# Spectral buffers lent to the end stage and to the second chunk pair, constant loads on SyncE's queue, and six free banks before a visit

## The chip, the cores and the metric

The kernel runs on one core of one Trainium2 chip. The time is device microseconds of one execution of the program, as the median over several runs. TensorE is called PE here, VectorE DVE, ScalarE ACT, GpSimd POOL and SyncE SP.

## What is computed

```python
g = sigmoid((q * gate_w).sum(-1, keepdims=True))
k_shift = causal convolution of k with 4 taps per channel
y = irfft(rfft(k_shift * v, 2S) * rfft(ssm_k, 2S))[:S] + k_shift * v * ssm_D
a = q * y
b = relu(q @ w1) @ w2
out = g * a + (1 - g) * b        # S = 2048, D = 512, DFF = 1792, float32
```

## The kernel before

Every float32 factor of the MLP is split into a high and a low part in the reduced format fp32r, and every product takes three matmuls (high by high, low by high, high by low). These are the dense matmuls: 128 x 128 weights against 512 columns. The 14 blocks of 128 hidden units are worked off in three eras (0 to 4, 5 to 9, 10 to 13), and in each era the 2048 rows go through in four chunks of 512. In the last era the chunks are taken in pairs (`combine(p, c, d, ...)`, chunks 0 and 1 for p = 0, chunks 2 and 3 for p = 1) and the first product of the MLP is done by a scheme with seven block products in place of eight; it needs sums and differences of the raw x of both chunks (`t1` to `t4`, on DVE), for which four pieces `b11`, `b12`, `b21`, `b22` of raw x are loaded, and `b22` a second time (`again`).

The long convolution is a two-stage Fourier transform. Its first stage (`stage1`, small-tile matmuls `s1h` and `s1x`) stores to the DRAM buffer `sa`. The middle (`conv_mid`) handles eight groups g: it loads `r_h` and `r_x` from `sa`, transforms both (`f_h`, `f_x`, 32 small-tile matmuls each in two halves of two PSUM banks), multiplies them on DVE into the spectral buffers `p`, `ha`, `qa`, `qb`, and adds the parts on POOL (`sums`, tile `p`; for g = 7 and part of g = 6 on DVE). The inverse `iv` of a group stands at the head of the visit two groups later and fills four banks; ACT copies these to `bv`, and SP stores them to the DRAM buffer `sb`. ACT also copies two of the four banks of `f_h` into `ha`. A visit is one such uninterrupted run of small-tile matmuls on PE between dense ones. The end (`conv_end`) is four more visits of 32 matmuls, `cy`, each in two halves; a half reads one pair of row blocks, loaded from `sb` into two `br` tiles of 512 KB each. DVE then forms g times q times `cy` (`after`) and adds the MLP's part (`finish`), and SP stores `out`.

The order of the instructions on each engine, and of the DMA issues on SP, is fixed when the program is built, by a list scheduler (`Plan`) with cost numbers of its own. Two of its rules matter here. A tile is given out from a counted set per tag (`room`), so that a load into a tag waits for whoever gave the buffer back. PSUM has eight banks, tag `cv`; the first link of a visit is taken only when `need` banks are free (`NEEDM`, five for every group g), or after it has waited `PATIENT` = 20 of the planner's microseconds. On the chip none of this is looked at again: an instruction waits only on the semaphores of the instructions whose data or buffers it uses.

SBUF is shared out by phases. Pool `cp1` serves stage one, `phase(2)` opens a pool with the spectral buffers (`p`, `ha`, `qa`, `qb`, `cf`, `cc`, `bv`), and `phase(3)`, which comes when all stores to `sb` and all gates are done, closes it and opens the pool with the `br` and `xs` tiles. `xs` holds the raw x of the second chunk pair.

The gates are computed by `gates`: a load of q, `tensor_tensor_reduce` with the gate weights `gwt` (in a `qb` buffer) and a scratch output `j` (in a `qa` buffer), and a sigmoid for eight row blocks at a time. Two constants, `s1t` (for stage one) and `ibt` (for `cy`), are loaded by DMAs that POOL issues at the start.

Of the kernel before, what the change touches and what calls it, by code (L numbers as in the profile page):

```python
# [11 lines left out]
OP = mybir.AluOpType  # L12

S, D, DFF = 2048, 512, 1792
P = 128
# [242 lines left out]
def dve_time(n):  # L258
    return n * 0.001042 + 0.12
# [3 lines left out]
TILES = 0.865  # L263
SWITCH = 0.19
ROW = P * D * 4


def build(tc, wf, xp, qn, kn, vn, hn, dn, sh, gw, w1, w2, cs1, ccf, cci, cib, out):
    nc = tc.nc
# [15 lines left out]
    room = {"raw": RAW, "x": 4, "cv": 8, "hh": HB, "cc": BEHIND + 1, "cf": 2, "qa": 1, "qb": 1, "acc": ACC, "tmp": TMP, "ev": EV, "r": RB,  # L285
            "ha": HAB, "p": PB, "bv": BVB, "j": 1, "w1": WA, "w2": WB, "br": BR, "xs": 4}
    plan = Plan(room)
# [135 lines left out]
    def combine(p, c, d, cgate):  # L423
        pairs = [tuple(ERAS[2][2 * u:2 * u + 2]) for u in range(2)]
        rank = (1, XR[p])
        tag = "xs" if p else "r"
        pool_of = lambda: cpool[0] if p else mp
        raws, made = {}, {}
        for nm, src, k0 in (("b22", d, 2), ("b12", d, 0), ("b11", c, 0), ("b21", c, 2)):
            go = lambda nm=nm, src=src, k0=k0: nc.sync.dma_start(rows(tile_of(("xc", p, nm), tag, 2 * D, p=pool_of())), xp[src, k0:k0 + 2].rearrange("k p d -> p k d"))  # L430
            raws[nm] = add("SP", ISSUE, -47, go, [cgate if p else xgate[0]], [tag], dma=2 * ROW, fifo=[tag])

# [26 lines left out]
        def again():  # L459
            nc.sync.dma_start(rows(tile_of(("xc", p, "b22"), tag, 2 * D, p=pool_of())), xp[d, 2:4].rearrange("k p d -> p k d"))  # L460

        for nm, ld in (("t2", "t4"), ("t3", "t2"), ("t4", "t4"), ("t1", "t2"), ("b22", None)):
            if not ld:
                made[ld] = add("SP", ISSUE, -47, again, [made["t2"]], [tag], dma=2 * ROW, fifo=[tag])
            for i in range(2):
                cut(nm, i, made[ld], [tag] if i else [])

# [77 lines left out]
        for u in us:  # L545
            relu(d, pairs[u][0], n("Y", u), c12[u], ["cv"])
        begun[0] = (p5 if LATE[p] else y)[1]
        for s in range(4):
            mlp2(2, d, s, [pairs[u][e] for e in (1, 0) for u in us])

# [197 lines left out]
    sbstores = []  # L748
    ys, rtags = {}, {}

# [18 lines left out]
    def conv_mid(g, gate):  # L769
# [37 lines left out]
        for o in range(2):  # L807
            f = link(TILES, lambda o=o: rounds("h", o), deps, ["cv"] * 2 + ([] if o else ["ha"]), rtags[g, "h"] if o else ())
            fh.append(f)
        if not IV_FIRST:  # L810
            turned()
# [85 lines left out]
    def gates(gate):  # L897
        rank = (1, GATE)

        def weights():  # L900
            nc.sync.dma_start(tile_of(("gwt",), "qb", 2 * D)[:, :D], gw.partition_broadcast(P))

        def junk():
            tile_of(("j",), "qa", 2 * D)
            tile_of(("gs",), "gs", 48, p=mp)

        gwl = add("SP", ISSUE, GATE - 1, weights, ys[7], ["qb"], dma=ROW)
        j = add("SP", 0.0, GATE - 1, junk, ys[7], ["qa"])
        done = []
        for m in range(0, 16, GN):  # L910
            prev = [None]
            for n in order_n[m:m + GN]:
                if n % 2 == 0:
                    def load(n=n):
                        two = tile_of(("gq", n), "r", 2 * D, p=mp)
                        nc.sync.dma_start(rows(two), qn[:, n:n + 2])
                        T["q", n], T["q", n + 1] = two[:, :D], two[:, D:]

                    ld = add("SP", ISSUE, GATE, load, [gate], ["r"], dma=2 * ROW, fifo=["r"])

                def go(n=n):
                    nc.vector.tensor_tensor_reduce(T["j",][:, :D], T["q", n], T["gwt",][:, :D], op0=OP.mult, op1=OP.add, scale=1.0, scalar=0.0, accum_out=gs(0, n))

                prev.append(add("DVE", dve_time(D) + 0.08, rank, go, [ld, gwl, j, *prev[-1:]], port=True))
            a = add("ACT", 0.2, rank, lambda m=m: nc.scalar.activation(gs(1, order_n[m], GN), gs(0, order_n[m], GN), AF.Sigmoid), prev[-1:])
            a = add("DVE", 0.07, rank, lambda m=m: nc.vector.tensor_scalar(gs(2, order_n[m], GN), gs(1, order_n[m], GN), -1.0, 1.0, op0=OP.mult, op1=OP.add), [a])
            for n in order_n[m:m + GN]:
                gdone[n] = a
# [4 lines left out]
    def conv_end(ns, gate):  # L933
        ready = {}
        for n in ns:
            rank = (1, 700.0 + order_n.index(n))
            k = lambda nm, n=n: (nm, n)

            if n % 2 == 0:
                def ld(n=n):  # L940
                    for b in range(2):
                        src = sb[64 * b:64 * b + 64].rearrange("(i n c) k d -> n (c k) i d", i=2, c=2)
                        nc.sync.dma_start(rows(tile_of(("br", b, n), "br", 2 * D)), src[n:n + 2].rearrange("n q i d -> (n q) i d"))

                e = add("SP", 2 * ISSUE, rank[1], ld, [gate], ["br", "br"], dma=4 * ROW, fifo=["br"])
            ready[n] = [e, gdone[n]]
        chain = []
        deps = [ibload] + [r[0] for r in ready.values()]
        for m in range(len(ns) // 2):
            def go(two=ns[2 * m:2 * m + 2]):  # L950
                for n in two:
                    bank(("cy", n))

                for to in range(4):
                    for n in two:
                        at = slice(64 * (n % 2), 64 * (n % 2) + 64)
                        mm(T["cy", n][32 * to:32 * to + 32, :], T["ibt",][at, :], T["br", to % 2, two[0]][at, to // 2 * D:(to // 2 + 1) * D], start=True, stop=True)  # L957

            chain.append(add("PE", TILES, (0, 700.0 + ns[0]), go, deps if not chain else chain[-1:], ["cv"] * 2, ["br", "br"], tiles=True, need=0 if chain else NEED))
            for n in ns[2 * m:2 * m + 2]:  # L960
                after(n, chain[-1], ready[n][1])
        plan.chain(chain)
# [21 lines left out]
    for k in range(4):  # L984
        load_x(0, 0, k, -1000 + k)
        load_first(k, -1002.5 + k)
    s1ld = add("POOL", 1.04, 0, lambda: nc.gpsimd.dma_start(tile_of(("s1t",), "s1c", 64), cs1), [w, p1], dma=ROW // 4)
    ibload = add("POOL", 1.04, 5, lambda: nc.gpsimd.dma_start(tile_of(("ibt",), "ibt", 32, p=mp), cib), [s1ld], dma=ROW // 8)
    for f in ERAS[0][G:]:
# [42 lines left out]
    gates(m2[1, CHUNKS[1][-1], 1])  # L1032
    p3 = add("SP", 0.0, -1e3, lambda: phase(3), sbstores + [gdone[n] for n in order_n])
    combine(1, *CHUNKS[2][2:], p3)
    for m in range(0, 16, NE):
# [14 lines left out]
NEED, PATIENT = 4, 20.0  # L1050
NEEDM = {g: 5 for g in range(8)}
NE = 4
# [5 lines left out]
GATE = 690.0  # L1058
BR = 8
LATE = True, False  # L1060
GN = 8
BACK = 1.5
CUT = (0, -899), (0, -899)
XR = 525.0, 704.5
WA = 7
# [73 lines left out]
```

## Time and profile before

| what | value |
|---|---|
| time, median of 3 runs | 383.59 us (383.54 to 383.60) |
| the profiled execution | 383.29 us, its span 381.5 us |
| PE busy | 376.6 us, 99% of the span |
| DVE busy | 299.2 us, 78% |
| ACT busy | 169.9 us, 45% |
| POOL busy | 82.4 us, 22% |
| granted clock | 1.000 of full speed |
| moved by DMA | 98.53 MB, mean 258 GB/s |

The profile is of one execution, whose time includes 1.79 us outside the span that the trace covers. PE, DVE, ACT and POOL count as busy while they execute; issuing a DMA does not count. An engine below 99% need not be free when it is wanted, and an idle one costs nothing unless PE waits for it.

### The profile page before, as it was taken

What the parts mean: (1) busy time and instruction counts of PE and PEld (TensorE: products, weight loads), DVE (VectorE), ACT (ScalarE), POOL (GpSimd) and SP (SyncE); (2) the same over time, 40 slices, a digit from 0 to 9 for tenths busy, and PEclk for the clock granted to TensorE, in tenths of its full rate; (3) what the DMA queues carried; (4) which work ended last, traced back from release to release, by engine and by line L of the source; (5) the groups of instructions that cost most, each with busy time, mean ns of one, the idle gap of its engine ahead of it and who ended that gap; (6) DMA issues with size and microseconds to landing.
All of it is one profiled execution on the core that took longest, in us unless ns stands there. A gap on an engine that the chain in (4) does not pass through costs nothing.

```text
span 381.5 us, 6622 instructions
## 1 busy us (share of the span) xinstructions
PE 376.6 (99%) x2481; PEld 265.3 (70%) x2481; DVE 299.2 (78%) x387; ACT 169.9 (45%) x311; POOL 82.4 (22%) x67
## 2 busy tenths in 40 slices
PE   9999999999999999999999999999999999999995
PEld 5888866866866886786646644657468688858664
DVE  5698999699599963127879898879899895699762
ACT  5542365275346644514132453053347864655230
POOL 1000000000000000000898899978400000000000
PEclk9999999999999999999999999999999999999999
DMA  8987178958958959789688979985753789159812
GB/s 276 381 314 246 55 284 317 338 201 317 365 195 305 338 213 346 257 278 327 236 298 285 304 221 368 326 281 174 262 207 113 246 298 380 38 187 320 293 58 82
DMA packets 45298, 98.53 MB, mean 258 GB/s; under 512 B 4657, under 2 KB 7489, under 8 KB 45266
## 3 DMA queue, kind: packets, MB, share of 16 engines
q1 hardware_dynamic: 44914, 97.80, 72.9%
q8 instruction: 19, 0.31, 0.3%
q10 hardware_dynamic: 288, 0.26, 0.2%
q14 instruction: 13, 0.11, 0.1%
q0 software_dynamic: 64, 0.05, 0.1%
HBM read 67.68 MB, written 30.41 MB: 257 GB/s over the span
## 4 chain that ended last, share of the span: by engine, by line
PE 98%; DMA 1%; DVE 0%; ACT 0%; DVEq 0%; issue 0%
PE m L628 14%; PE m L629 13%; PE m L630 13%; PE m L412 9%; PE m L413 9%; PE m L414 9%; PE iv L865 4%; PE f_x L786 4%; PE f_h L786 4%; PE m L398 3%; PE s1x L673 2%; PE X L486 2%; PE cy L957 2%; PE X L487 2%; PE X L488 2%; PE s1h L673 2%
## 5 line engine op out<-in xcount | busy, mean ns | idle before, releaser
L628 PE MATMUL m<-w1h_h,hh 128*128 128x512 f32 x224 | 89.1, 398 | 0.0
L629 PE MATMUL m<-w1l_l,hh 128*128 128x512 f32 x224 | 87.3, 390 | 0.0
L630 PE MATMUL m<-w1h_h,hl 128*128 128x512 f32 x224 | 87.2, 389 | 0.0
L837 POOL TENSOR_TENSOR p<-p,ha 128x512 f32<-128x512 f32 x26 | 33.1, 1297 | 184.4 <-DVE ha L831 183.9
L628 PEld LDWEIGHTS m<-w1h_h,hh 128*128 128x128 f32 x224 | 42.0, 188 | 21.5 <-ACT ev L678 6.5
L602 ACT ACTIVATE hh<-m 128x512 fp32r<-128x512 f32 x40 | 23.6, 599 | 65.8 <-PE m L414 65.8
L630 PEld LDWEIGHTS m<-w1h_h,hl 128*128 128x128 f32 x224 | 42.0, 188 | 9.0
L629 PEld LDWEIGHTS m<-w1l_l,hh 128*128 128x128 f32 x224 | 42.1, 188 | 8.2
L605 DVE SCALAR_TENSOR_TENSOR hl<-m,hh 128x512 fp32r<-128x512 f32 x40 | 27.2, 686 | 24.5 <-ACT hh L602 24.5
L412 PE MATMUL m<-xh_h,w0h_h 128*128 128x512 f32 x96 | 37.7, 393 | 0.0
L413 PE MATMUL m<-xl_l,w0h_h 128*128 128x512 f32 x96 | 37.4, 389 | 0.0
L414 PE MATMUL m<-xh_h,w0l_l 128*128 128x512 f32 x96 | 37.4, 389 | 0.0
L875 ACT COPY bv<-iv 128x512 f32<-128x512 f32 x32 | 18.1, 598 | 40.3 <-PE iv L865 39.7
L643 ACT COPY y<-m 128x512 f32<-128x512 f32 x28 | 16.5, 590 | 38.5 <-PE m L630 38.2
L732 DVE TENSOR_TENSOR acc<-acc,tmp 128x1024 f32<-128x1024 f32 x24 | 29.4, 1224 | 0.8
L412 PEld LDWEIGHTS m<-xh_h,w0h_h 128*128 128x128 f32 x96 | 18.0, 188 | 6.2 <-issue 1.7
L729 DVE TENSOR_TENSOR tmp<-r,sht_sht 128x512 f32<-128x512 f32 x32 | 20.8, 684 | 0.2
L678 ACT COPY ev<-s1x 128x512 f32<-128x512 f32 x32 | 16.4, 600 | 9.4 <-PE s1x L673 9.4
L414 PEld LDWEIGHTS m<-xh_h,w0l_l 128*128 128x128 f32 x96 | 18.0, 188 | 3.8
L413 PEld LDWEIGHTS m<-xl_l,w0h_h 128*128 128x128 f32 x96 | 18.0, 188 | 3.6
L823 DVE TENSOR_TENSOR ha<-f_h,ha 128x512 f32<-128x512 f32 x16 | 10.6, 688 | 12.6 <-PE f_h L786 11.6
L837 POOL TENSOR_TENSOR p<-p,qa 128x512 f32<-128x512 f32 x14 | 20.3, 1466 | 0.0
(147 smaller groups left out, 659.9 us busy)
## 6 DMA issues: line engine op xcount, KB each, us to landing
sa<-ev SPq DMA_DIRECT2D x64, 256.0 KB, 3.0
r_h<-sa SPq DMA_DIRECT2D x16, 512.0 KB, 5.5
r_x<-sa SPq DMA_DIRECT2D x16, 512.0 KB, 6.8
sb<-bv SPq DMA_DIRECT2D x32, 256.0 KB, 2.6
br<-sb SPq DMA_DIRECT2D x16, 512.0 KB, 7.3
raw<-xp SPq DMA_DIRECT2D x28, 256.0 KB, 4.0
raw<-w SPq DMA_DIRECT2D x22, 256.0 KB, 3.9
r<-kn SPq DMA_DIRECT2D x10, 512.0 KB, 5.0
```

The source lines that it names most:

```text
L412: mm(ps, part("h", f, k), T["x", "h", xe, c, k], start=k == 0, stop=False)
L413: mm(ps, part("h", f, k), T["x", "l", xe, c, k], start=False, stop=False)
L414: mm(ps, part("l", f, k), T["x", "h", xe, c, k], start=False, stop=k == 3)
L602: nc.scalar.activation(tile_of(("hh", era, c, f), "hh", dt=F32R, p=mp, bufs=HB), T["m1", era, c, f], AF.Relu)
L605: nc.vector.scalar_tensor_tensor(tile_of(("hl", era, c, f), "hl", dt=F32R, p=mp, bufs=HB), T["m1", era, c, f], 0.0, T["hh", era, c, f].bit ...
L628: mm(ps, T["hh", era, c, f][:, z], T["w", "h", 1, f], start=f == fs[0] and not seeding, stop=False, skip_group_check=True)
L629: mm(ps, T["hh", era, c, f][:, z], T["w", "l", 1, f], start=False, stop=False, skip_group_check=True)
L630: mm(ps, T["hl", era, c, f][:, z], T["w", "h", 1, f], start=False, stop=f == fs[-1], skip_group_check=True)
L729: nc.vector.tensor_tensor(o[:, z], T["k", c + (j == 0) + part][:, u], T["sht",][:, j * D:(j + 1) * D], op=OP.mult)
L732: nc.vector.tensor_tensor(T["acc", c], T["acc", c], T[dst], op=OP.add)
L786: mm(ps[b][32 * j:32 * j + 32, :], T[k("cf")][at, 64 * j + 32 * o:64 * j + 32 * o + 32], T[k("r", t, j // 2)][at, (j % 2) * D:(j % 2 + 1) ...
L837: (nc.gpsimd if eng == "POOL" else nc.vector).tensor_tensor(planes("p", dst, n), planes("p", dst, n), planes(src, u, n), op=OP.add if sign ...
```

## The change

The pool of the spectral buffers is no longer closed before the end stage. The pairs of row blocks that `conv_end` loads go, in turn, into `p`, `p`, a buffer `bx` of its own, `p`, `p`, `bx`, `ha`, `ha`, and the raw x of the second chunk pair into the two `ha` tiles (two pieces each) and the second `b22` into `qa`; these loads are gated by group 7's `f_h` and not by `phase(3)`. The gate weights and the scratch output have tiles of their own. The two constant loads are issued by SP, and the scratch memory for DMAs that GpSimd describes is set to 2048. `NEEDM` is six. `EARLY` = 2, 2 takes the place of `LATE`: for both pairs, the first two of the four accumulators of the second chunk may be seeded from the earlier of two points.

```diff
@@ -283,7 +283,7 @@
 
 
     room = {"raw": RAW, "x": 4, "cv": 8, "hh": HB, "cc": BEHIND + 1, "cf": 2, "qa": 1, "qb": 1, "acc": ACC, "tmp": TMP, "ev": EV, "r": RB,
-            "ha": HAB, "p": PB, "bv": BVB, "j": 1, "w1": WA, "w2": WB, "br": BR, "xs": 4}
+            "ha": HAB, "p": PB, "bv": BVB, "j": 1, "w1": WA, "w2": WB, "bx": 1}
     plan = Plan(room)
     add = plan.add
     T = Tiles()
@@ -423,12 +423,22 @@
     def combine(p, c, d, cgate):
         pairs = [tuple(ERAS[2][2 * u:2 * u + 2]) for u in range(2)]
         rank = (1, XR[p])
-        tag = "xs" if p else "r"
-        pool_of = lambda: cpool[0] if p else mp
         raws, made = {}, {}
+        home = dict(b22=0, b12=0, b11=1, b21=1)
         for nm, src, k0 in (("b22", d, 2), ("b12", d, 0), ("b11", c, 0), ("b21", c, 2)):
-            go = lambda nm=nm, src=src, k0=k0: nc.sync.dma_start(rows(tile_of(("xc", p, nm), tag, 2 * D, p=pool_of())), xp[src, k0:k0 + 2].rearrange("k p d -> p k d"))
-            raws[nm] = add("SP", ISSUE, -47, go, [cgate if p else xgate[0]], [tag], dma=2 * ROW, fifo=[tag])
+            def go(nm=nm, src=src, k0=k0):
+                if not p:
+                    tile_of(("xc", p, nm), "r", 2 * D, p=mp)
+                else:
+                    if nm in ("b22", "b11"):
+                        tile_of(("xt", home[nm]), "ha", 4 * D)
+                    T["xc", p, nm] = T["xt", home[nm]][:, 2 * D * (nm in ("b12", "b21")):][:, :2 * D]
+                nc.sync.dma_start(rows(T["xc", p, nm]), xp[src, k0:k0 + 2].rearrange("k p d -> p k d"))
+
+            if p:
+                raws[nm] = add("SP", ISSUE, -47, go, [cgate, *raws.values()], ["ha"] if nm in ("b22", "b11") else (), dma=2 * ROW)
+            else:
+                raws[nm] = add("SP", ISSUE, -47, go, [xgate[0]], ["r"], dma=2 * ROW, fifo=["r"])
 
         def minus(dst, a, b, deps, into, sign=-1):
             def go(eng="DVE"):
@@ -457,13 +467,13 @@
         minus("t4", "b21", "t2", [made["t2"], raws["b21"], *own("b21")], "b21")
 
         def again():
-            nc.sync.dma_start(rows(tile_of(("xc", p, "b22"), tag, 2 * D, p=pool_of())), xp[d, 2:4].rearrange("k p d -> p k d"))
+            nc.sync.dma_start(rows(tile_of(("xc", p, "b22"), "qa" if p else "r", 2 * D, p=None if p else mp)), xp[d, 2:4].rearrange("k p d -> p k d"))
 
         for nm, ld in (("t2", "t4"), ("t3", "t2"), ("t4", "t4"), ("t1", "t2"), ("b22", None)):
             if not ld:
-                made[ld] = add("SP", ISSUE, -47, again, [made["t2"]], [tag], dma=2 * ROW, fifo=[tag])
+                made[ld] = add("SP", ISSUE, -47, again, [made["t2"], *(ys[7] if p else ())], ["qa" if p else "r"], dma=2 * ROW, fifo=() if p else ["r"])
             for i in range(2):
-                cut(nm, i, made[ld], [tag] if i else [])
+                cut(nm, i, made[ld], ["r"] if not p and i else {"t4": ["ha"], "t1": ["ha"], "b22": ["qa"]}.get(nm, []) if i else [])
 
         def x_at(b, nm, i):
             if not p and nm in ("b21", "b11"):
@@ -544,8 +554,8 @@
         c12 = [summed(n("Y", u), n("Y", u), n("u2", u), [y[u]], ["raw"]) for u in us]
         for u in us:
             relu(d, pairs[u][0], n("Y", u), c12[u], ["cv"])
-        begun[0] = (p5 if LATE[p] else y)[1]
         for s in range(4):
+            begun[0] = (p5 if s < EARLY[p] else y)[1]
             mlp2(2, d, s, [pairs[u][e] for e in (1, 0) for u in us])
 
     wpart = {}
@@ -746,7 +756,7 @@
 
 
     sbstores = []
-    ys, rtags = {}, {}
+    ys, rtags, fh7 = {}, {}, [None]
 
     def conv_load(g, gate):
         rank = 500.0 + 4 * g
@@ -807,6 +817,7 @@
         for o in range(2):
             f = link(TILES, lambda o=o: rounds("h", o), deps, ["cv"] * 2 + ([] if o else ["ha"]), rtags[g, "h"] if o else ())
             fh.append(f)
+        fh7[0] = fh[0]
         if not IV_FIRST:
             turned()
 
@@ -898,14 +909,11 @@
         rank = (1, GATE)
 
         def weights():
-            nc.sync.dma_start(tile_of(("gwt",), "qb", 2 * D)[:, :D], gw.partition_broadcast(P))
-
-        def junk():
-            tile_of(("j",), "qa", 2 * D)
+            nc.sync.dma_start(tile_of(("gwt",), "gwt", p=mp), gw.partition_broadcast(P))
+            tile_of(("j",), "j", p=mp)
             tile_of(("gs",), "gs", 48, p=mp)
 
-        gwl = add("SP", ISSUE, GATE - 1, weights, ys[7], ["qb"], dma=ROW)
-        j = add("SP", 0.0, GATE - 1, junk, ys[7], ["qa"])
+        gwl = add("SP", ISSUE, GATE - 1, weights, [gate], dma=ROW)
         done = []
         for m in range(0, 16, GN):
             prev = [None]
@@ -919,9 +927,9 @@
                     ld = add("SP", ISSUE, GATE, load, [gate], ["r"], dma=2 * ROW, fifo=["r"])
 
                 def go(n=n):
-                    nc.vector.tensor_tensor_reduce(T["j",][:, :D], T["q", n], T["gwt",][:, :D], op0=OP.mult, op1=OP.add, scale=1.0, scalar=0.0, accum_out=gs(0, n))
-
-                prev.append(add("DVE", dve_time(D) + 0.08, rank, go, [ld, gwl, j, *prev[-1:]], port=True))
+                    nc.vector.tensor_tensor_reduce(T["j",], T["q", n], T["gwt",], op0=OP.mult, op1=OP.add, scale=1.0, scalar=0.0, accum_out=gs(0, n))
+
+                prev.append(add("DVE", dve_time(D) + 0.08, rank, go, [ld, gwl, *prev[-1:]], port=True))
             a = add("ACT", 0.2, rank, lambda m=m: nc.scalar.activation(gs(1, order_n[m], GN), gs(0, order_n[m], GN), AF.Sigmoid), prev[-1:])
             a = add("DVE", 0.07, rank, lambda m=m: nc.vector.tensor_scalar(gs(2, order_n[m], GN), gs(1, order_n[m], GN), -1.0, 1.0, op0=OP.mult, op1=OP.add), [a])
             for n in order_n[m:m + GN]:
@@ -931,18 +939,23 @@
     gs = lambda i, n, m=1: T["gs",][:, 16 * i + order_n.index(n):16 * i + order_n.index(n) + m]
 
     def conv_end(ns, gate):
-        ready = {}
+        ready, tags = {}, {}
         for n in ns:
             rank = (1, 700.0 + order_n.index(n))
             k = lambda nm, n=n: (nm, n)
 
             if n % 2 == 0:
-                def ld(n=n):
+                tag = "p p bx p p bx ha ha".split()[order_n.index(n) // 2]
+
+                def ld(n=n, tag=tag):
+                    two = tile_of(("br", n), tag, 4 * D, p=mp if tag == "bx" else None)
                     for b in range(2):
+                        T["br", b, n] = two[:, 2 * D * b:2 * D * b + 2 * D]
                         src = sb[64 * b:64 * b + 64].rearrange("(i n c) k d -> n (c k) i d", i=2, c=2)
-                        nc.sync.dma_start(rows(tile_of(("br", b, n), "br", 2 * D)), src[n:n + 2].rearrange("n q i d -> (n q) i d"))
-
-                e = add("SP", 2 * ISSUE, rank[1], ld, [gate], ["br", "br"], dma=4 * ROW, fifo=["br"])
+                        nc.sync.dma_start(rows(T["br", b, n]), src[n:n + 2].rearrange("n q i d -> (n q) i d"))
+
+                e = add("SP", 2 * ISSUE, rank[1], ld, [gate], [tag], dma=4 * ROW, fifo=["brs"])
+                tags[n] = tag
             ready[n] = [e, gdone[n]]
         chain = []
         deps = [ibload] + [r[0] for r in ready.values()]
@@ -956,7 +969,7 @@
                         at = slice(64 * (n % 2), 64 * (n % 2) + 64)
                         mm(T["cy", n][32 * to:32 * to + 32, :], T["ibt",][at, :], T["br", to % 2, two[0]][at, to // 2 * D:(to // 2 + 1) * D], start=True, stop=True)
 
-            chain.append(add("PE", TILES, (0, 700.0 + ns[0]), go, deps if not chain else chain[-1:], ["cv"] * 2, ["br", "br"], tiles=True, need=0 if chain else NEED))
+            chain.append(add("PE", TILES, (0, 700.0 + ns[0]), go, deps if not chain else chain[-1:], ["cv"] * 2, [tags[ns[2 * m]]], tiles=True, need=0 if chain else NEED))
             for n in ns[2 * m:2 * m + 2]:
                 after(n, chain[-1], ready[n][1])
         plan.chain(chain)
@@ -984,8 +997,8 @@
     for k in range(4):
         load_x(0, 0, k, -1000 + k)
         load_first(k, -1002.5 + k)
-    s1ld = add("POOL", 1.04, 0, lambda: nc.gpsimd.dma_start(tile_of(("s1t",), "s1c", 64), cs1), [w, p1], dma=ROW // 4)
-    ibload = add("POOL", 1.04, 5, lambda: nc.gpsimd.dma_start(tile_of(("ibt",), "ibt", 32, p=mp), cib), [s1ld], dma=ROW // 8)
+    s1ld = add("SP", ISSUE, -29.5, lambda: nc.sync.dma_start(tile_of(("s1t",), "s1c", 64), cs1), [w, p1], dma=ROW // 4)
+    ibload = add("SP", ISSUE, 5, lambda: nc.sync.dma_start(tile_of(("ibt",), "ibt", 32, p=mp), cib), [s1ld], dma=ROW // 8)
     for f in ERAS[0][G:]:
         load_w(0, f, -100 + f)
     for f in ERAS[0]:
@@ -1030,8 +1043,8 @@
     order_n = [4 * c + s for c in CHUNKS[2] for s in range(4)]
     combine(0, *CHUNKS[2][:2], None)
     gates(m2[1, CHUNKS[1][-1], 1])
-    p3 = add("SP", 0.0, -1e3, lambda: phase(3), sbstores + [gdone[n] for n in order_n])
-    combine(1, *CHUNKS[2][2:], p3)
+    p3 = add("SP", 0.0, -1e3, lambda: None, sbstores)
+    combine(1, *CHUNKS[2][2:], fh7[0])
     for m in range(0, 16, NE):
         conv_end(order_n[m:m + NE], p3)
 
@@ -1048,7 +1061,7 @@
 DEBUG = None
 DIRECT = 3,
 NEED, PATIENT = 4, 20.0
-NEEDM = {g: 5 for g in range(8)}
+NEEDM = {g: 6 for g in range(8)}
 NE = 4
 XW = 512.0
 PREP = 42.0, 43.0
@@ -1056,12 +1069,11 @@
 ALT = 0
 DSUM = {7: tuple(range(8)), 6: (6, 7)}
 GATE = 690.0
-BR = 8
-LATE = True, False
+EARLY = 2, 2
 GN = 8
 BACK = 1.5
 CUT = (0, -899), (0, -899)
-XR = 525.0, 704.5
+XR = 525.0, 695.0
 WA = 7
 SHARE = 0.0
 LONG = 50.0, 50.0, 0.0, 0.0
@@ -1129,7 +1141,7 @@
         "cib": ib,
     }
     arrays = {k: np.ascontiguousarray(v, np.float32) for k, v in arrays.items()}
-    nc = bacc.Bacc("TRN2", target_bir_lowering=False, num_devices=1)
+    nc = bacc.Bacc("TRN2", target_bir_lowering=False, num_devices=1, dynamic_dma_scratch_size=2048)
     aps = [nc.dram_tensor(k, v.shape, F32, kind="ExternalInput").ap() for k, v in arrays.items()]
     out = nc.dram_tensor("out", (P, 16, D), F32, kind="ExternalOutput").ap()
     with tile.TileContext(nc) as tc:
```

The order on PE, at the visit in which group 5 goes forward and group 3 back (only the rows of `f_h` and `f_x` that wait; the names are bank_half_group). Before:

```order
L786 MATMUL f_h_0_0_5_2525<-r_h_0_5_2253,cf_5_2287 32x512 [waits DMAHW6_49,DMAHW1_49,DVE_49]
...
L786 MATMUL f_h_1_0_5_2542<-r_h_0_5_2253,cf_5_2287 32x512 [waits Activation_49]
L786 MATMUL f_h_1_1_5_2543<-r_h_0_5_2253,cf_5_2287 32x512 [waits DVE_49]
...
L786 MATMUL f_x_0_0_5_2556<-r_x_0_5_2306,cf_5_2287 32x512 [waits DMAHW3_49,Activation_49]
...
L786 MATMUL f_x_1_0_5_2573<-r_x_0_5_2306,cf_5_2287 32x512 [waits Activation_49]
```

And of the change:

```order
L796 MATMUL f_h_0_0_5_2579<-r_h_0_5_2297,cf_5_2366 32x512 [waits DMAHW7_49,DVE_49]
...
L796 MATMUL f_h_1_0_5_2596<-r_h_0_5_2297,cf_5_2366 32x512 [waits DVE_49]
L796 MATMUL f_h_1_1_5_2597<-r_h_0_5_2297,cf_5_2366 32x512 [waits PE_49]
...
L796 MATMUL f_x_0_0_5_2612<-r_x_0_5_2389,cf_5_2366 32x512 [waits DMAHW1_49,Activation_49]
...
L796 MATMUL f_x_1_0_5_2629<-r_x_0_5_2389,cf_5_2366 32x512 [waits PE_49,Activation_49]
L796 MATMUL f_x_1_1_5_2630<-r_x_0_5_2389,cf_5_2366 32x512 [waits PE_49]
```

Before, the second half of `f_h` takes a bank that ACT frees (copy `bv_0`) and the two halves of `f_x` take banks freed by ACT's two copies of `f_h` itself; now `f_h` takes banks that were free ahead of the visit, and `f_x` takes those of the copies `bv_1` and `bv_2`. The visit of group 6 reads alike; group 3 read so before, and now waits as group 5 did. PE has as many matmuls and as many visits as before; the number of dense matmuls ahead of each visit changes from the first full visit on (before, in the place where the orders part: 24, 27, 30, 30, 33, 63, 30, 69, 156, 21, 51, 33, 48; now: 36, 39, 39, 33, 36, 36, 66, 96, 87, 27, 33, 54, 33; the eighth stands ahead of the inverse of group 7, the ninth ahead of the first `cy`, the last is the tail).

SP's queue where the end stage's loads are issued (a name of `br` is half_row block). Before:

```order
L430 DMA xs_1_b21_3429<-xp 128x2x512 [waits DMAHW7_49]
L943 DMA br_0_0_3439<-sb_67 128x2x512 [waits DMAHW2_49,DMAHW1_49,DMAHW0_49]
...
L943 DMA br_0_6_3540<-sb_67 128x2x512 [waits DMAHW6_49]
L943 DMA br_1_6_3542<-sb_67 128x2x512 [waits DMAHW7_49]
L460 DMA xs_1_b22_3584<-xp 128x2x512 [waits DMAHW0_49,DVE_49]
L892 DMA out<-r_0_2989 128x512 [waits DMAHW1_49,DVE_49]
L892 DMA out<-r_0_2989 128x512 [waits DMAHW2_49,DVE_49]
L943 DMA br_0_8_3620<-sb_67 128x2x512 [waits DMAHW3_49,PE_49]
L943 DMA br_1_8_3622<-sb_67 128x2x512 [waits DMAHW4_49,PE_49]
```

And of the change, with names tag_row block:

```order
L955 DMA p_0_3447<-sb_67 128x2x512 [waits DMAHW2_49,DMAHW1_49,DMAHW6_49,DMAHW0_49,DMAHW7_49,PE_49,Pool_49]
L955 DMA p_0_3447<-sb_67 128x2x512 [waits DMAHW3_49]
L470 DMA qa_1_b22_3471<-xp 128x2x512 [waits DMAHW4_49]
L955 DMA p_2_3479<-sb_67 128x2x512 [waits DMAHW5_49,PE_49]
L955 DMA p_2_3479<-sb_67 128x2x512
L955 DMA bx_4_3508<-sb_67 128x2x512 x2
L955 DMA p_6_3575<-sb_67 128x2x512 [waits DMAHW3_49,DMAHW2_49,PE_49]
L955 DMA p_6_3575<-sb_67 128x2x512
L903 DMA out<-r_0_2992 128x512 [waits DVE_49]
L903 DMA out<-r_0_2992 128x512 [waits DMAHW4_49,DVE_49]
L955 DMA p_8_3615<-sb_67 128x2x512 [waits DMAHW6_49,DMAHW5_49,PE_49]
```

Before, four pairs (row blocks 0 to 7) were loaded ahead and the fifth, `br_8`, was the first to wait for PE; now the fourth (`p_6`) waits for PE, which is the first half of the first `cy`, and the fifth for its second half.

ACT's queue around the inverse of group 6, as the change has it (before, that inverse stood among the dense matmuls of the era before, and no copy of its banks stood here):

```order
L512 COPY raw_0_0_3132<-X_0_0_3010 128x512 [waits DVE_49,PE_49]
L886 COPY bv_0_6_3144<-iv_0_6_3112 128x512 [waits DMAHW0_49,PE_49]
L886 COPY bv_1_6_3146<-iv_1_6_3113 128x512 [waits DMAHW1_49,PE_49]
L334 CAST xh_h_0_t4_0_3153<-r_0_b21_2863 128x512 [waits DMAHW5_49,PE_49]
L886 COPY bv_2_6_3159<-iv_2_6_3114 128x512 [waits DMAHW3_49]
L512 COPY raw_0_1_3162<-X_0_1_3020 128x512 [waits DVE_49,PE_49]
L334 CAST xh_h_0_t4_1_3170<-r_0_b21_2863 128x512
L512 COPY raw_0_0_3175<-X_0_0_3010 128x512 [waits DVE_49,PE_49]
L886 COPY bv_3_6_3178<-iv_3_6_3115 128x512 [waits DMAHW4_49]
```

The inverse now stands between the products with `t2` of the two hidden pairs, so four copies of its banks come between ACT's copies to `raw`, which the products with `t3` and `t4` wait for.

## Rows read from the trace of the kernel before

**Rows 1.** The page: busy time of each engine, share of the span, instructions.

```profile
PE 376.6 (99%) x2481; PEld 265.3 (70%) x2481; DVE 299.2 (78%) x387; ACT 169.9 (45%) x311; POOL 82.4 (22%) x67
```

**Rows 2.** The page: the chain that ended last, by engine.

```profile
PE 98%; DMA 1%; DVE 0%; ACT 0%; DVEq 0%; issue 0%
```

**Rows 3.** That chain in order of time (start us, us, what): both ends.

```profile
4.53 11.30 PE m L398 x48
...
374.11 0.23 PE m L628
...
377.29 0.24 PE m L630
```

**Rows 4.** The same chain: the visits of groups 3 and 4.

```profile
207.31 1.90 PE iv L865 x32
209.21 1.88 PE f_h L786 x32
211.09 1.72 PE f_x L786 x32
...
219.83 1.90 PE iv L865 x32
221.73 1.88 PE f_h L786 x32
223.61 1.99 PE f_x L786 x32
```

**Rows 5.** Waits (engine, line, waited for, us in total, times, longest).

```profile
PEld f_x L786 <- ACT ha L818: 8.1, 10, 0.8
```

**Rows 6.** ACT in the visit of group 4 (start, us, line, operation).

```profile
221.83 1.07 ACT L875 COPY bv<-iv 128x512 f32<-128x512 f32 x2 [0.67 <-ACT xh_h L334]
222.89 0.59 ACT L818 COPY ha<-f_h 128x512 f32<-128x512 f32 x1
223.37 0.59 ACT L875 COPY bv<-iv 128x512 f32<-128x512 f32 x1
223.85 0.60 ACT L818 COPY ha<-f_h 128x512 f32<-128x512 f32 x1
```

**Rows 7.** POOL at the start: the first of its two DMA issues.

```profile
1.25 0.68 POOL L987 DMA_DIRECT2D s1c_s1t<-cs  x1 [0.80 <-POOLq L1132]
```

**Rows 8.** The tile `br`: all 16 loads, duration of the issue in ns, and landing.

```profile
L943 SPq DMA_DIRECT2D br<-sb x16: 360/462/1390, 308.4 to 355.4; - x16
DMA to landing us min/median/max: 4.5/7.3/10.1
```

**Rows 9.** The chain: the inverses of groups 6 and 7, the first two end visits.

```profile
279.16 1.90 PE iv L865 x32
...
296.94 1.90 PE iv L865 x32
298.84 0.43 PE X L486
...
334.43 1.88 PE cy L957 x32
...
341.29 1.88 PE cy L957 x32
```

**Rows 10.** The tile `sb`, the last store of `bv`: its issue, and its landing.

```profile
L872 SPq DMA_DIRECT2D sb<-bv x1: 320/320/320, 303.5 to 303.5; - x1
DMA to landing us min/median/max: 2.0/2.0/2.0
```

**Rows 11.** The tile `br`, 339 to 341 us: the fifth pair.

```profile
DMA to landing us min/median/max: 5.7/5.9/6.2
```

**Rows 12.** The tile `br`, 345.5 to 347 us: the seventh pair.

```profile
DMA to landing us min/median/max: 9.0/9.4/9.8
```

**Rows 13.** ACT behind the inverse of group 6.

```profile
281.17 2.06 ACT L875 COPY bv<-iv 128x512 f32<-128x512 f32 x4 [9.69 <-PE iv L865]
...
284.06 0.62 ACT L334 CAST xh_h_t<-r_b 128x512 fp32r<-128x512 f32 x1
```

## The prediction

> **What bounds the kernel now.** I read the totals first. PE is busy 376.6 us, 99% of the 381.5 us span, while DVE has 78% and ACT 45% [rows 1]. The chain of waits says the same: 98% of it is PE [rows 2]. So the time is a sum along one engine: PE starts its real work at 4.53, ends its last matmul at 377.5, and 4.0 us of finish and store follow it [rows 3]. A change can gain only by taking time out of PE's own sequence, at its start, or behind its last matmul; it can lose wherever it makes PE wait.
>
> PE's sequence is dense matmuls at 0.227 us each (fourteen starts lie between 374.11 and 377.29 [rows 3]), cut by visits of the convolution. A visit that runs an inverse, f_h and f_x takes 1.90 + 1.88 + f_x. Here the visits differ: f_x of g=3 takes 1.72, of g=4 1.99 [rows 4]. Among the six full visits g=3 is the only short one; g=2, 4, 5, 6 and 7 are long, and the two without an inverse (g=0, 1) are short. The difference, 0.27 us, has a name in the list of waits: f_x waits for ACT's copy of f_h into ha, ten times, two per long visit [rows 5]. ACT's timeline at g=4 shows why: the eight banks hold four of the inverse and four of f_h, ACT empties bv, bv, ha, bv, ha in that order, and f_x starts when the first ha copy, begun at 222.89, has ended [rows 6].
>
> **The change, part by part.** The executed time is 383.29 us for the profiled run, 1.79 us more than its span; the median of the runs is 383.59, 0.30 above it. I sum against 383.29 and add the 0.30 at the end.
>
> *Six free banks.* It alters the build-time order, not an instruction. PE has the same number of matmuls, and the same number of visits: nothing is taken out except waits. In the order I followed each bank's last reader. In g=5 and g=6, f_x now waits for the second bv copy and the third, and for no ha copy; these two visits go from 1.99 to 1.72, 2 x 0.27 = 0.54 us gained. g=3, short before, now waits for both ha copies: ACT has one bv copy fewer ahead of them, but in g=4 the first ha copy started only 0.10 us after ACT could have taken it (two copies 0.48 apart from 221.83 leave it free at 222.79, and ha began at 222.89, so f_h itself was the later one [rows 6]); I give back the whole 0.27. g=2, 4 and 7 keep their ha waits. Sum: −0.27 us.
>
> The Trainium skill (TensorEngine Tiling (Array Packing), "PSUM Bottleneck") says that tiling speeds TensorE up but not the copies out of PSUM, which can then become the bottleneck. The trace agrees: ten waits, 8.1 us of weight-load idleness, stand on ACT's copies. By that rule alone the visits would stay ACT's and the gain would be 0, not −0.27; a rival below has that case.
>
> *Constant loads from POOL to SP.* POOL spends 0.68 us on the first of them, and less on the second, before any work of its own [rows 7]; its next work comes far later, so nothing is saved there. On SP they cost two issues of about 0.4 us in a queue that is at that point ahead of PE; the cover is the dense work up to the first small-tile visit, and I see no stall in the first 50 us. Without POOL's DMAs the end has two completions fewer to check, somewhere in the 4.0 us between PE's end and the span's; no row parts them out, so I take 0, bounds 0 and −0.2. The smaller scratch only frees memory: 0.
>
> *Own tiles for gwt and j.* Gates can start earlier and DVE's work moves, with no instruction added on PE: 0 while DVE stays below full; it is 78% busy.
>
> *Raw x of the second pair into ha.* Loads that went into a new pool after phase(3) now go as soon as ha is free; they are needed some 10 us later than they can land. 0; its loss would need a landing above the slowest end-stage load, 10.1 us [rows 8].
>
> *End-stage loads in lent buffers.* In the order, dense matmuls ahead of the first and the second end visit become 6 and 12 more, so these start at 334.43 + 1.36 = 335.8 and 341.29 + 2.72 = 344.0 [rows 9]. The inverse of g=7 moves to 87 dense matmuls before the first: it ends near 335.8 − 0.2 − 19.75 = 315.9 (the 0.2 is what the first matmul behind a visit takes longer, 0.43 against 0.23), against 298.84 before. The last store of bv landed 2.0 us after issue, 6.7 us after that inverse ended (303.5 + 2.0 − 298.84) [rows 9, 10], so the loads can start near 322.5. Five loads must land before 335.8. One pair issued after a pause took 5.7 to 6.2 us [rows 11], one behind another pair 9.0 to 9.8 [rows 12], and none over 10.1 [rows 8]. At 0.46 us an issue [rows 8] the fifth goes out at 324.3 and at the slowest lands at 334.4, 1.4 us early. 0.
>
> The fourth pair is the sharp point. It takes the buffer of the first pair, so it can be issued only after the first half of the first end visit: 335.8 + 0.94 + some 0.2 = 336.9, its second half at 337.4. The second end visit needs it in its second half, 344.0 + 0.94 = 344.9. With the quiet rows it lands at 337.4 + 6.2 = 343.6, 1.3 us early; with the heavy ones at 337.4 + 9.8 = 347.2, 2.3 us late; with the slowest, 2.6 us late. I take the quiet rows, since those were also issued behind a pause of SP, and here the third pair is the only load ahead, issued 10 us before. So 0, bounds 0 and +2.6. What queues behind it on SP are two out stores and the fifth pair, not needed before the third end visit near 353.6. The sixth pair has the same tie to the second visit, from 345.1 to 354.5 some 9 us, about what the heavy rows take.
>
> The Trainium skill (DMA: Bandwidth & Descriptors, "Anatomy of one DMA") gives about 2.0 us plus bytes / 436e3 for a DMA issued by GpSimd; an estimate from it for 512 KB is 3.2 us, with which the fourth pair would land near 340.6. No row here is that short: the shortest of these loads took 4.5 us.
>
> *ACT around the inverse of g=6.* This visit now stands between two products of the first chunk pair (48 dense matmuls later: 279.16 + 10.9 = 290.1, ending 292.0 [rows 9]). ACT has two bv copies, a cast and a third bv ahead of the copy to raw that the thirteenth matmul behind the visit needs, at 292.0 + 0.2 + 2.72 = 294.9. Four bv copies took 2.06 us, a pitch of 0.49, a cast 0.62 [rows 13]. So bv at 292.1 and 292.6, cast 293.1, bv 293.6, the copy 294.1 to 294.7: 0.2 us to spare. 0, bounds 0 and +0.6 (one more copy ahead).
>
> *Sum.* −0.27: 383.02 for the profiled run, 383.32 for the median. I say 383.3. What a measurement of this kernel can tell from no change is 0.2%, 0.77 us, so the likeliest verdict is no difference. Range of this case: 382.8 to 383.6.
>
> **The rivals.** *All visits become short:* if the earlier-freed banks also spare the ha waits in g=2, 3, 4 and 7, five visits lose 0.27: −1.35, 382.2 to 382.3. For it: the waits are few and equal. Against it: the order still names the ha copies there.
>
> *The visits do not shorten:* with ACT's copies as the bound, f_x of g=5 and g=6 starts no sooner, waiting for bv copies just as late. Short g=3 speaks against it, since its f_x waited for the same bv copies. If so, 0 and perhaps +0.27 from g=3: 383.6 to 383.9.
>
> *The fourth pair is late:* decided at a landing of 7.5 us from the second issue; half of the 16 loads took 7.3 or more [rows 8]. For it: the range of those rows; out stores in the same queue. Against it: the load is nearly alone. Price up to +2.6, so 383.3 to 385.9, 384.6 in the middle: slower than before.
>
> *ACT is late at the inverse of g=6,* or another product of the moved stretch waits for DVE or ACT: +0.2 to +1.0, 383.4 to 384.3. PE had no stall there before; the new order has margins of 0.2 us.
>
> **How the numbers follow.** Likeliest 0.50; visits do not shorten 0.10; all short 0.12; fourth pair late 0.16 (of it two thirds beyond +0.77 net); ACT or DVE late 0.12 (a third beyond). Faster: 0.12 for all short, and 0.05 for a gain at the start or end that I do not see. Slower: 0.11 + 0.04 + 0.03 of the case with g=3 lost. Same: the rest, 0.65. The range runs from 382.0, the lowest rival with some margin, to 385.0, which cuts off the slowest landings.
>
> **What would show it.** In the changed profile: f_x at 1.72 in g=5 and g=6 and 1.99 in g=2, 4 and 7; in the list of waits f_x behind ha eight times in place of ten; PE's last matmul near 377.0; no end visit with idle PE ahead; the fourth pair's load landing by 344.9; no wait of X for the copy to raw behind the inverse of g=6. The prediction is wrong if PE idles between 290 and 345, or if a visit ends much earlier than its copies.

## The result and the profile after

The changed kernel takes 384.74 us (median of 6 runs, 384.63 to 385.12) against 383.56 us of the kernel before beside it (6 runs, 383.15 to 383.85): a ratio of 1.0035, interval 1.0022 to 1.0048. It is slower by 1.2 us. The forecast was no measurable difference, 383.3; the time lies inside the outer range, 382.0 to 385.0, but above the range of the likeliest case, 382.8 to 383.6, and on the side that had the chance 0.18. All medians are of fast runs: one run each of b_nosums (541.52), pooldma (2155.85) and the kernel before (1339.54) is left out. The profiled execution took 384.69 us, its span 382.9.

The page after, busy time and chain, to be set beside [rows 1, 2]:

```profile
PE 376.5 (98%) x2481; PEld 265.8 (69%) x2481; DVE 302.3 (79%) x389; ACT 169.9 (44%) x311; POOL 79.1 (21%) x63
...
PE 98%; DVE 1%; ACT 0%; DVEq 0%; issue 0%
```

PE does the same work in a longer span, and 1% of the chain is now DVE's, 1.9 us of it in the two DVE rows below. The chain in order of time shows where (start us, us, what):

```profile
288.14 0.24 PE V L498
288.38 0.02 issue
288.40 0.60 ACT hh L516
289.00 0.52 ACT xh_h_t L334
289.52 1.28 DVE w1l_l L337 x2
290.79 0.61 DVE hl L519
291.41 0.14 issue
291.54 1.98 PE iv L876 x32
```

PE ends a product at 289.6 and starts the inverse of group 6 at 291.54. By the gaps between its matmuls it loses 1.89 us there (2.21 from the last matmul's start to the next, where a switch without a wait takes 0.32) and, but for `f_x` of g=3 (below), waits nowhere else behind the first microseconds where the kernel before did not. The list of waits names the releaser: the inverse needs four banks, and one of them still held V of hidden tile 10, which DVE's `hl` reads last (the last line; its columns are the wait, us in total, times, longest).

```profile
PEld f_x L796 <- ACT ha L829: 6.5, 8, 0.8
...
PE iv L876 <- DVE hl L519: 1.8, 1, 1.8
```

The first line answers to [rows 5]: eight waits in place of ten, as forecast. The visits do so too: g=3 has become long, g=5 and g=6 short (chain; the first two rows are `iv` and `f_x` of g=3, to be set beside [rows 4], the last two `f_x` of g=5 and g=6).

```profile
212.68 1.90 PE iv L876 x32
...
216.46 2.01 PE f_x L796 x32
...
244.79 1.72 PE f_x L796 x32
...
258.67 1.72 PE f_x L796 x32
```

The sum for the profiled run: 383.29 − 0.27 (visits) + 1.89 (the wait) − 0.2 (from PE's end to the span's end, 3.8 us in place of 4.0) = 384.71, measured 384.69.

Why was `hl` late? DVE after, from the end of group 6's multiplications to `hl` (start, us, line, operation):

```profile
269.02 8.18 DVE L446 TENSOR_TENSOR r_b<-r_b,r_b 128x1024 f32<-128x1024 f32 x4
277.12 1.28 DVE L834 TENSOR_TENSOR ha<-f_h,ha 128x512 f32<-128x512 f32 x2
278.50 2.29 DVE L842 TENSOR_TENSOR p<-f_x,ha 128x2048 f32<-128x2048 f32 x1
...
288.31 0.69 DVE L337 TENSOR_TENSOR w1l_l<-raw,w1h_h 128x512 fp32r<-128x512 f32 x1
288.91 0.69 DVE L648 TENSOR_TENSOR y<-m,y 128x512 f32<-128x512 f32 x1
289.51 1.28 DVE L337 TENSOR_TENSOR w1l_l<-raw,w1h_h 128x512 fp32r<-128x512 f32 x2
290.71 0.69 DVE L519 SCALAR_TENSOR_TENSOR hl<-V,hh 128x512 fp32r<-128x512 f32 x1
```

ACT had finished `hh`, which `hl` needs, by 287.64; DVE came to it three microseconds later, having run without a pause since 267.3. Its four subtractions (`t1` to `t4` of the first chunk pair) took 8.18 us. POOL ran its last four sums of group 6 in the same stretch:

```profile
268.15 3.51 POOL L848 TENSOR_TENSOR p<-p,qa 128x512 f32<-128x512 f32 x2
271.62 4.49 POOL L848 TENSOR_TENSOR p<-p,qb 128x512 f32<-128x512 f32 x2
```

Two such sums take 2.5 us elsewhere in the trace. So each engine stretches the other. In the kernel before, DVE started the same `hl` at 290.14, only 0.6 us earlier, but there it was not late: `hh` had ended no sooner than 290.10. The first row is ACT's `hh` of the change, the others are of the kernel before.

```profile
287.04 0.60 ACT L516 ACTIVATE hh<-V 128x512 fp32r<-128x512 f32 x1
...
289.50 0.60 ACT L506 ACTIVATE hh<-V 128x512 fp32r<-128x512 f32 x1 [1.42 <-PE V L488]
290.14 0.68 DVE L509 SCALAR_TENSOR_TENSOR hl<-V,hh 128x512 fp32r<-128x512 f32 x1
```

Nobody waited then: PE's products V ended at 290.8 and not at 288.4, because the inverse of group 6 and its 2.1 us stood ahead of the products (at 279.2) and not behind them; the other 0.3 us are the visits. Up to here the reading of two traces; the experiments test it.

### The profile page after: what moved, and what is told of

Its sections match the earlier page's. It is cut to its first block, busy times and chain, and to the rows that moved or that the text cites. A ratio compares the mean times of both kernels' runs of the same rounds, so it can differ in the third digit from the quotient of the medians.

```text
span 382.9 us, 6634 instructions
## 1 busy us (share of the span) xinstructions
PE 376.5 (98%) x2481; PEld 265.8 (69%) x2481; DVE 302.3 (79%) x389; ACT 169.9 (44%) x311; POOL 79.1 (21%) x63
## 4 chain that ended last, share of the span: by engine, by line
PE 98%; DVE 1%; ACT 0%; DVEq 0%; issue 0%
PE m L638 14%; PE m L639 13%; PE m L640 13%; PE m L412 9%; PE m L413 9%; PE m L414 9%; PE iv L876 4%; PE f_h L796 4%; PE f_x L796 4%; PE m L398 3%; PE s1x L683 2%; PE cy L970 2%; PE X L496 2%; PE s1h L683 2%; PE X L497 2%; PE X L498 2%
## 5 line engine op out<-in xcount | busy, mean ns | idle before, releaser
L848 POOL TENSOR_TENSOR p<-p,ha 128x512 f32<-128x512 f32 x26 | 34.0, 1325 | 196.8 <-DVE ha L842 196.3
L337 DVE TENSOR_TENSOR xl_l<-raw,xh_h 128x512 fp32r<-128x512 f32 x28 | 20.9, 792 | 0.0
L848 POOL TENSOR_TENSOR p<-p,qb 128x512 f32<-128x512 f32 x14 | 20.6, 1498 | 0.0
```

Of the source, the lines that this page charges most:

```text
L337: (nc.gpsimd if eng == "POOL" else nc.vector).tensor_tensor(tile_of(lo, tag + "l", dt=F32R, bufs=bufs, p=p), T[key], T[hi].bitcast(F32), o ...
L848: (nc.gpsimd if eng == "POOL" else nc.vector).tensor_tensor(planes("p", dst, n), planes("p", dst, n), planes(src, u, n), op=OP.add if sign ...
```

## The experiments

Each is set against runs of the kernel before, taken beside it: 383.44 us for need5, need6, nosums and hlfirst, 383.74 for late_x, sums6, fix and pooldma, 383.62 for place and b_nosums.

**need5**: the changed kernel with one number set back.

```diff
-NEEDM = {g: 6 for g in range(8)}
+NEEDM = {g: 5 for g in range(8)}
```

> The changed kernel with five free banks in place of six, all else as changed. Theory 1 (the six banks move the inverse of group 6 to where it waits 1.9 us for DVE): the visits stand as before the change up to that inverse, no idle PE ahead of it, one short visit (g=3); time 383.5 to 383.7, the same as before. Rival (the lent buffers and earlier loads crowd DVE and the DMA queues, the banks have no part): the idle PE near 290 stays or moves, and the time stays near 384.7.

Measured 383.57 us, ratio 1.000 (0.9991 to 1.001). The inverse of group 6 starts at 279.20, PE does not wait ahead of it, g=3 is the only short full visit. Without the six banks the whole rest of the change (lent buffers, early raw x, the constant loads on SP, `EARLY`, the rank `XR`) costs and gains nothing that can be measured.

**need6**: the kernel before, with six in place of five.

> The kernel before with six free banks and nothing else of the change. Theory 1: the order of PE up to the inverse of group 6 is that of the change, two short visits (g=5, 6) gain 0.27 net and PE idles 1.9 us ahead of that inverse, so 384.7 to 385.2. Rival (the buffers do it): no idle PE there, 383.2 to 383.5.

Measured 392.43 us, ratio 1.0236 (1.0217 to 1.0255). Theory 1 had the order right, and the wait ahead of the inverse of group 6 is there (1.5 us), but the expectation missed by 7 us: behind the inverse of group 7 comes a second wait. The chain (start, us, what):

```profile
321.13 1.98 PE iv L865 x32
...
325.64 0.50 ACT bv L875
...
326.57 0.38 SPq L430
...
327.04 4.95 DMA xs_b<-xp
...
332.12 1.23 DVE xs_b L436
...
333.42 1.23 DVE xs_b L436
334.64 0.61 DVE xl_l_b L337
...
336.09 0.43 PE X L488
336.52 0.43 PE X L486
```

With the inverse of group 7 at 321 in place of 297, the pool of the end stage opens only then, and the raw x of the second chunk pair, which was loaded into it, comes too late for the first product. PE is idle from 329.9 to 334, its second product then waits for its low part until 335.3, and its matmuls come 0.43 us apart until 340. So the change's parts belong together: the early raw x takes away most of what the six banks alone would cost.

**late_x**: the changed kernel, raw x of the second pair gated as before.

```diff
-    combine(1, *CHUNKS[2][2:], fh7[0])
+    combine(1, *CHUNKS[2][2:], p3)
```

> The changed kernel with the raw x of the second chunk pair loaded only behind the last stores to sb, as before the change; six banks and lent buffers stay. If the early raw x is what the change gains against the six banks alone (392.4), PE idles 4 us or more for that raw x or for the first pairs behind the inverse of group 7, 387 to 393. Rival (the lent br buffers are what matters): within 0.5 us of the change, 384.3 to 385.2.

Measured 394.45 us, ratio 1.0283 (1.0261 to 1.0306), above the expected range by 1.5. The wait is there: `ha<-xp` landed 8.16 us after its issue at 326, and the first product of the second pair went on at 336.2. PE also waited 0.6 us for the loads `p<-sb` inside the first end visit, and part of the 10 us is matmuls at half speed (last section). The lent `br` buffers alone do not help; the early raw x does.

**nosums**: POOL's last four sums of group 6 left out, so `p` of that group lacks four of its terms.

```diff
             def go():
+                if g == 6 and src in ("qa", "qb"):
+                    return
```

> The changed kernel without POOL's last four sums of group 6 (p with qa, p with qb), which leaves them out of the result; every other instruction in the same order. Theory 2 (DVE is late because the four 1024-wide subtractions of the first chunk pair run beside these sums and take 8.18 us): they take 4 x 1.22 = 4.9 us, DVE is 3.3 us earlier, PE does not wait ahead of the inverse of group 6, 382.8 to 383.0. Rival (DVE simply has too much in that stretch, or the order of its queue does it): the subtractions take 8 us also without POOL, or PE waits still, 384.3 to 384.8.

Measured 383.08 us, ratio 0.999 (0.9981 to 0.9999), 0.1 above the range of theory 2. DVE's subtractions and `hl`:

```profile
269.78 4.99 DVE L446 TENSOR_TENSOR r_b<-r_b,r_b 128x1024 f32<-128x1024 f32 x4
...
288.42 0.69 DVE L519 SCALAR_TENSOR_TENSOR hl<-V,hh 128x512 fp32r<-128x512 f32 x1
290.39 0.68 DVE L337 TENSOR_TENSOR xl_l_t<-r_b,xh_h_t 128x512 fp32r<-128x512 f32 x1
```

4.99 in place of 8.18, and PE's wait is gone. (This execution's first matmuls came 0.427 us apart from 5.0 to 6.3, which shifts everything behind by 0.7 us against the changed kernel's trace.) The collision of the two engines is shown; whether it alone is to blame was still open.

**hlfirst**: only the place of `hl` in DVE's queue.

```diff
     issued = plan.order()
+    later = [wdone[1, f] for f in (10, 11, 12)]
+    issued = [o for o in issued if not any(o is w for w in later)]
+    at_h = [o is hdone[2, 0, 10] for o in issued].index(True)
+    issued[at_h + 1:at_h + 1] = later
```

> The changed kernel with one move in DVE's queue: the three splits w1l of hidden tiles 10 to 12 stand behind the hl of tile 10 in place of ahead of it. Theory 1 (the inverse waits for that hl alone): hl starts at 288.9 in place of 290.7, the idle PE of 1.9 us falls to 0.1 or less, 382.8 to 383.0, faster than before by 0.6. Rival (another instruction is late next, the copy to raw on ACT or a y that frees a bank): PE waits 0.5 us or more in the same stretch, 383.3 to 384.3.

Measured 384.57 us, ratio 1.0031 (1.0018 to 1.0043), 0.3 above the rival's range. The rival's mechanism came true: `hl` started at 288.96 and the wait ahead of the inverse fell to 0.1 us, but the products with `t4` now waited 0.67 and 0.41 us for their low parts. The chain there:

```profile
295.59 0.60 DVE p L848
296.19 0.27 DVE xl_l_t L337
...
296.70 0.68 DVE p L848
297.39 0.61 DVE xl_l_t L337
298.00 0.04 issue
298.05 0.50 PE X L497
```

So it is not one instruction in the wrong place. DVE is late for the whole stretch.

**place**: the inverse of group 6 one product later on PE, and ACT's two copies to `raw` ahead of its `bv` copies.

```diff
     issued = plan.order()
+    at_iv = [o["eng"] == "PE" and o["rank"] == (0, 1, 532.0) and len(o["take"]) == 4 for o in issued].index(True)
+    moved = [o for o in issued[at_iv:] if o["eng"] == "PE" and o["rank"] in ((1, 71, 1, 0), (1, 71, 1, 1)) or o["eng"] == "ACT" and o["rank"] == (0, -929)]
+    issued = [o for o in issued if not any(o is m for m in moved)]
+    issued[at_iv:at_iv] = moved
```

> The changed kernel with the inverse of group 6 one product later on PE (the two matmul triples of X with t2 of the second hidden pair stand ahead of it), and ACT's two copies to raw ahead of its bv copies; DVE's queue as it is. Theory 3 (DVE is late for the whole stretch, wherever the inverse stands): PE waits about 0.5 us ahead of the inverse and again at the products with t4, whose splits come at 296.7 and 297.9, so only 0.5 to 0.9 us is won, 383.9 to 384.3. Rival (the place of the inverse alone does it): the wait falls to 0.5 us or less and none comes behind, 383.0 to 383.4.

Measured 384.51 us, ratio 1.0028 (1.0018 to 1.0038). The rival falls. Theory 3 has the waits (0.5 ahead of the inverse, 0.4 and 0.3 at the products with `t4`), and won 0.2 us by the medians, less than it said: the time is 0.2 above its range.

**b_nosums**: the same four sums left out of the kernel before.

> The kernel before without POOL's last four sums of group 6, which leaves them out of the result; PE's order unchanged. Theory 3: there too the subtractions run beside these sums (7.0 us), and DVE's lateness is just covered, since the products of the first pair are needed 2 us later: nothing is won, 383.4 to 383.7, the same. Rival (the collision costs time before the change too): 383.0 or less.

Measured 383.41 us, ratio 0.9998 (0.9989 to 1.0008). Nothing is won there, as theory 3 says. The test is weaker than nosums: one subtraction still took 2.31 us beside another POOL instruction.

**sums6**: the last two sums of group 6 on POOL, which takes 1.2 us off DVE ahead of `hl`.

```diff
-                (nc.gpsimd if eng == "POOL" else nc.vector).tensor_tensor(
+                on_pool = eng == "POOL" or (g == 6 and src == "ha" and u < 2)
+                (nc.gpsimd if on_pool else nc.vector).tensor_tensor(
```

> The changed kernel with the last two sums of group 6 on POOL in place of DVE, nothing else moved. Theory 2 (DVE runs without a gap from 267 on, so each us taken off it ahead of the hl of hidden tile 10 comes off PE's wait): DVE is 1.2 us earlier, the idle PE ahead of the inverse of group 6 falls from 1.9 to 0.7, 383.4 to 383.7. Rival (the sums on POOL, 2.5 us and later, hold the inverse of group 6 or stretch DVE again): 384.5 or more.

Measured 383.87 us, ratio 1.000 (0.9991 to 1.0009), 0.2 above the expected range. PE's wait ahead of the inverse is 0.68 us: the 1.2 us that come off DVE come off the wait, one for one.

**fix**: sums6 and hlfirst together.

> The changed kernel with both: the last two sums of group 6 on POOL, and the three splits w1l behind the hl of hidden tile 10. Theory 2: the splits alone moved the wait to the products with t4 (0.7 + 0.4 us); with DVE 1.2 us earlier there is no wait left either there or ahead of the inverse, 382.9 to 383.2, faster than before by 0.3 to 0.6. Rival (another engine is next, ACT's copy to raw): a wait of 0.3 us or more remains near 290 to 298, 383.4 or more.

Measured 383.16 us, ratio 0.999 (0.998 to 0.9999). No wait above 0.1 us is left ahead of the inverse of group 6 or at the products behind it. The inverse of group 6 and the end visits, to be set beside [rows 9]:

```profile
289.71 1.90 PE iv L877 x32
...
335.72 1.88 PE cy L971 x32
343.94 1.88 PE cy L971 x32
```

The end visits start at the 335.8 and 344.0 that the prediction worked out for a sequence without waits. This version beats the changed kernel by about 1.6 us and the kernel before by 0.1%, just clear of the interval: 383.16 against 383.74, where the prediction's −0.27 and the −0.2 of the end make −0.5.

**pooldma**: the changed kernel with the two constant loads issued by POOL, as before.

> The changed kernel with the two constant loads issued by POOL again. The part costs nothing: 384.6 to 384.9, the same as the change, PE's wait of 1.9 us ahead of the inverse of group 6 unchanged. Rival (two completions fewer at the end are a gain): the time from PE's end to the span's end is 0.2 us longer, 384.9 to 385.0; or DVE's new order of stage one adds a wait there.

Measured 385.05 us, ratio 1.0036 (1.0024 to 1.0049): the same as the change, though above the range expected. The rival about the end holds in the trace: the stretch from PE's end (378.8) to the span's end (382.8) is 4.0 us, against 3.8 in the change; the times do not resolve 0.2 us. PE's wait ahead of the inverse was 1.5 us in this execution and not 1.9, as DVE reached `hl` 0.3 us sooner, at 290.4.

## Why the prediction was wrong

- **Right:** the bound (PE's sequence), the two visits made short and the one made long (−0.27, 1.72 and 1.99 to 2.01 in the trace), three that stay long. The two rivals about them fell: not all visits became short, and they did shorten.
- **Right:** the end stage at 0. The sharp point, the fourth pair, was issued at 338.5 and 338.9 and landed 6.0 us later, at 344.9, where the quiet rows had said 6.2; the second end visit began at 345.6 and needed it in its second half.

```profile
L955 SPq DMA_DIRECT2D p<-sb x2: 360/416/472, 338.5 to 338.9; - x2
...
DMA to landing us min/median/max: 6.0/6.0/6.0
```

- **Right in size, taken as 0:** the end without POOL's DMAs, −0.2 at the bound named. All four kernels that issue the two loads from POOL (before, need6, b_nosums, pooldma) have an end 0.2 us longer in their traces than the other eight. Behind the last landing SP goes through its remaining waits 0.06 us apart, seven in the kernel before and five in the change, which makes 0.12 of the 0.2; the rest was not followed.
- **Wrong:** the step "ACT around the inverse of g=6", put at 0, and with it "0 while DVE stays below full; it is 78% busy". The step followed what stands behind the inverse (ACT's copies; no wait came there in fix) and did not ask what the inverse itself waits for: a bank that DVE gives back. It should have been: the inverse moves behind two products, so V of hidden tile 10 comes 2.4 us earlier on PE (288.4 for 290.8) and its `hh` at 287.6 for 290.1, while DVE reaches `hl` only at 290.7, where it had been at 290.1. That is +1.9. The busy share over the span hid it: DVE had no pause from 267 to 298.
- The rival "ACT is late at the inverse of g=6, or another product of the moved stretch waits for DVE or ACT" had the place, with a chance of 0.12, and a price of at most 1.0 where 1.9 was measured.
- **Luck:** that the time lies inside the outer range. Its upper end, 385.0, was there for a late fourth pair, which landed in time; the rival with the right place ended at 384.3.

That DVE was behind at all comes from the subtractions beside POOL's sums, 3.2 us, which nosums shows. The trace of before had the same collision (those four subtractions took 1.2 to 2.2 us each), and the prediction did not look at it, because nothing waited for DVE there:

```profile
260.27 1.55 DVE L436 TENSOR_TENSOR r_b<-r_b,r_b 128x1024 f32<-128x1024 f32 x1
...
263.44 1.21 DVE L436 TENSOR_TENSOR r_b<-r_b,r_b 128x1024 f32<-128x1024 f32 x1
...
265.18 4.27 DVE L436 TENSOR_TENSOR r_b<-r_b,r_b 128x1024 f32<-128x1024 f32 x2
```

The Trainium skill (SBUF — State Buffer, "SBUF: two separate sides") says that a DVE instruction with two inputs from SBUF and a GpSimd instruction that reads SBUF take the shared port in turns, each for its whole length. The trace agrees in the main: DVE's subtractions, both of whose inputs are in SBUF, and POOL's sums took about 8 us side by side and some 5 us each without the other, while multiplications with one input from PSUM kept their 1.2 us beside POOL. In turns for their whole length a subtraction and a sum would take 1.2 + 1.3 = 2.5 us; side by side they came every 2.2 us, and that is the number to go by.

How much place won: its waits, 1.2 in place of 1.9, promise 0.7 us, but the first matmul behind a wait takes 0.11 us longer (0.34 for 0.23), and place has two such waits more. In its trace PE's sequence from the visit of group 7 to the inverse of that group is 0.5 us shorter than in the change. The medians show 0.2; the intervals allow either.

## What to carry to other kernels

When a change moves a block of work to a later place on the bounding engine, everything between its old and its new place comes earlier by the block's length; follow each buffer that the block takes to the instruction that frees it, and read from the trace when that instruction ran, not when its inputs were ready. An engine without slack that nobody waits for is invisible in the waits of the kernel before, so look for stretches where it has no pause, and not at its share of the span. When a wait is removed by moving one instruction, look whether it comes back at the next: moving alone did not remove it here, only time taken off the late engine did (nosums), or that with the move (fix).

## What the runs showed of the hardware

After a wait of 4 us PE came back slowly, after one of 1.9 us it did not. In need6 PE was idle from 329.9 to 334 and again for 0.9 us until 335.3, and its matmuls then came 0.43 us apart until 340, with 0.23 on either side. The windows view (us, then busy time and number of each engine, the granted clock, the DMA share and GB/s) has a mean granted clock of 0.71 from 329 to 340, a mixture of its two levels, 1.2 and 2.4 GHz (from 334 to 340 it is 0.50):

```profile
329.00:340.00 11.00, 6.56 (x17) 4.59 (x16) 7.22 (x8) 3.43 (x6) 0.00 (x0) 0.71 1.04 389
```

So a part of need6's 9 us, some 2 us, is matmuls at half speed and not the wait itself. In the changed kernel the clock stayed at 1.00 through the wait of 1.9 us. The length of a single wait did not decide it: in late_x PE waited about 1 us at most at a time between 330 and 336.2, and 1.4 us at 340.4, and its matmuls came 0.43 us apart from 336.2 to 339.6 and again from 343.5 to 346.4, at a granted clock of 0.51 and 0.50, which is the level of 1.2 GHz. The view has both in a longer stretch, with a mean of 0.90:

```profile
317.00:350.00 33.00, 29.25 (x163) 18.52 (x148) 19.58 (x32) 14.37 (x27) 0.00 (x0) 0.90 0.85 298
```
